# Placing the first expert block ahead of the third pair's last attention outputs, with the first half's gather plan put earlier

## The chip, the core and the metric

One NeuronCore of a Trainium2 chip runs the whole program in one launch. The metric is the device time of that launch in microseconds (us). Five instruction streams run side by side and meet through semaphores: PE (TensorE, matrix products), DVE (VectorE), ACT (ScalarE), POOL (GpSimd, which also issues the indirect transfers) and SP (SyncE, which issues all the other transfers).

## What is computed

Eight batches of 576 tokens go through linear attention with 8 heads, then through a mixture of 8 experts of which each token uses two, then through a soft mixture of experts.

```python
kv = np.einsum('bhsd,bhde->...', softmax(k, over tokens), v)   # per head 64x64
x  = softmax(q, over dims) @ kv                                 # 4608 x 512
...
noisy = x @ w_gate + log1p(exp(x @ w_noise)) * noise            # 4608 x 8
top2, weights = two largest per token, softmax over the two
out[mask] += weight * (relu(x[mask] @ w1[e]) @ w2[e])           # each expert e
...
soft mixture of experts over out                                # second stage
```

The weights `w1[e]` are 512 x 1024 and `w2[e]` 1024 x 512, in float32. A product in float32 is made of three products: each operand is split into a high and a low part, and high x high, high x low and low x high are summed.

## The kernel before

**Attention.** The tokens are taken in four pairs of batches (`i` = 0 to 3), each of nine tiles of 128 tokens (`j` = 0 to 8). The order of the work is written by hand as two tables of short steps. `FIRST` is run before the expert stage, `MIX` is spread over the first nine blocks of the expert stage (`SPREAD = 72` parts, eight parts to a block). A step is two letters and its numbers: `lk`, `lv`, `lq` load; `km` to `ke` make the softmax of k; `kv` forms k^T v and `kb`, `kt`, `ku`, `kw`, `kx` turn it into the tile `KB`; `qm`, `qs`, `qe` make exp(q - max) of three tiles (`qs` on GpSimd, with a `v` behind it on VectorE); `qt` and `qu` transpose one tile of q into `qT`; `ou` is the product of `qT` with `KB` into the PSUM tile `pv`; `os`, `oa`, `ol` or `ov` scale it into `xr` and `lgr`; `st` stores 128 rows into the DRAM table `xtab`; `he` sums the gate logits over the heads. `ga` starts the gate of a pair (or of two) as a background generator, and each `bg` runs one piece of it. The gate ends in `tab`, which holds for every expert the numbers of its tokens.

**Order.** Inside `FIRST` every engine runs its instructions in the order of the table (`tc.manual_schedule`). In `MIX` and in the expert stage a scheduler places the instructions of each engine when the program is built; it may take one ahead of another on the same engine where no data forbids it.

**First half's plan.** After the gates of pairs 0 and 1, `plan_first` (L633) turns the counts and `tab` into the list of rows for the first ten expert blocks: `pl_m` (L594 to L597), the counts (L639 to L654), eight copies on GpSimd into `pl_ia` at places that are read into registers (L656), the expert of each block `pl_eba` (L629) and `pl_done` (L665). Then two indirect transfers (`gather_rows`, L774) fetch the 2 x 128 rows of block 0 into `pl_x0` and `pl_x1`. The second half's plan (`plan`, step `pl`) is the last step of `MIX` but for its `bg`s; its row lists `pl_idx` and `pl_id3` are copied on GpSimd (L735 to L744).

**Expert blocks.** A block is 256 gathered rows and one expert. SP reads the expert's number (`expert`, L814) and loads eight pieces of 512 KB of its weights into `ringS` (L819; u = 0 to 3 are `w1`, 4 to 7 `w2`). Each piece is split by ACT into its high part `R?h` and by DVE into its low part `R?l` (`split`, L827), in three slots R0, R1, R2 taken in turn. `xpose` (L847 to L852) transposes the rows on PE, ACT makes `xh`, DVE makes `xl` and the weight of each row (`sc`). `hidden` (L862) makes 24 products of 256 columns for each of u = 0 to 3, and ACT and DVE make `hh` (L865) and `hl` (L866). `result` (L892) makes 12 products of 512 columns for each of u = 4 to 7. DVE scales the two results into `y` (L897) and GpSimd adds them to `x2` by an indirect transfer (L898). Weights and rows of the next block are fetched during the block; its rows are transposed at u = 6.

PSUM for `pv` has two buffers (`pb`, `pc`) during `FIRST` and one (`pb`) after it; the PSUM of the expert stage takes the place of `pc` and of the three transpose buffers.

Blocks 0 to 9 take rows of the first half. After them come blocks of three tiles (`THREE`) and of two, whose number is read at run time.

Of the kernel before, what the change touches and what calls it, by code (L numbers as in the profile page):

```python
# [59 lines left out]
kv3.1.0 bg st2.5 ke3.0.1 bg kv3.1.1 bg ov2.2 bg ou2.8 bg st2.2 he2.0 bg qt2.3 ov2.8 bg qu2.3 ou2.4 bg st2.8 bg kb3.1 bg kv3.0.0 bg pf bg kt3.1 kv3.0.1 ku3.1 kw3.1 kx3.1 kb3.0 bg os2.4 ou2.7 qm3.0   # L60
oa2.4 kt3.0 ov2.7 ou2.3 ku3.0 st2.4 ol2.4 qm3.1 qs3.0 st2.7 kw3.0 ou2.6 kx3.0 os2.3 qs3.2v oa2.3 qs3.1 ov2.6 qe3.0 st2.3 he2.2v st2.6 ol2.3 qe3.2 he2.1 qe3.1
# [66 lines left out]
def attention(k):  # L128
# [3 lines left out]
    with ExitStack() as ctx:  # L132
# [440 lines left out]
        plain = {"lk": load_k, "lv": load_v, "lq": load_q, "se": setup, "wu": level, "kf": rest_tr, "kg": rest_max, "km": k_max, "kn": km_tr, "ko": km_max, "kp": ms_tr, "ks": k_sub, "ke": k_exp, "qe": q_exp, "qt": q_tr, "qu": q_copy, "kb": kv_out, "kt": kb_tr, "ku": kb_copy, "kw": kb_w, "kx": kw_copy, "ou": out, "os": out_sums, "ol": out_logits, "st": out_store}  # L573
# [59 lines left out]
def plan_first(k, cnt):  # L633

    nc = k.nc
    t = lambda n, s, d=F32: k.ac.tile(s, d, name=n)
    m = table(k)
    pn = k.pt([P, E])
    nc.tensor.matmul(pn, k.ones16, cnt, start=True, stop=True)  # L639
    k.c1 = t("pl_c1", [P, E])  # L640
    nc.vector.tensor_copy(k.c1, pn)
    ti = t("pl_ti", [P, E], I32)
    nc.vector.tensor_copy(ti, pn)
    nc.vector.tensor_scalar(ti, ti, 8, None, op0=ALU.logical_shift_right)
    cf = t("pl_tf", [P, E])
    nc.vector.tensor_copy(cf, ti)
    ru = t("pl_ru", [P, 2, E + 1, E])[:, 0]
    nc.vector.tensor_tensor(ru, bcast(cf, 1, E + 1), k.tri, op=ALU.mult)
    en = t("pl_en", [P, 2, E + 1])[:, 0]
    nc.vector.tensor_reduce(en, ru, axis=AX.X, op=ALU.add)  # L650
    st = t("pl_st", [P, E], I32)
    nc.vector.tensor_scalar(st, en[:, :E], 2.0, None, op0=ALU.mult)
    k.idxa = k.cp.tile([P, TE + TE], I32, name="pl_ia")
    nc.vector.memset(k.idxa, 0)  # L654
    for e in range(E):
        nc.gpsimd.tensor_copy(k.idxa[:, bass.ds(at_register(k, st[0:1, e:e + 1], TE), TE)], m[:, e * TE:(e + 1) * TE])  # L656
    k.eoha = k.cp.tile([P, NPA, E], F32, name="pl_eoa")
# [813 lines left out]
```

## Time and profile before

| | |
|---|---|
| median of 3 runs | 1192.28 us (1190.68 to 1193.77) |
| profiled execution | 1193.88 us, its span 1192.2 us |
| mean granted clock of PE, as a share of full speed | 0.971 |
| PE busy | 1116.4 us, 94% of the span |
| DVE, ACT, POOL busy | 67%, 48%, 28% of the span |
| HBM traffic | 242 GB/s over the span |

The profile is of one execution. A row of a timeline gives the start, the duration, the engine, the line of the kernel, the operation with its output and inputs, the count of instructions merged in the row, and in brackets the idle time before it with what ended it. PE's products in float32 appear as two records each. A `windows` row gives for a stretch the busy time of each engine and how many instructions, PE's granted clock (1.00 is 2.4 GHz, 0.50 is 1.2 GHz), the share of the 16 DMA engines and GB/s.

### The profile page before, as it was taken

What the parts mean: (1) busy time and instruction counts of PE and PEld (TensorE: products, weight loads), DVE (VectorE), ACT (ScalarE), POOL (GpSimd) and SP (SyncE); (2) the same over time, 40 slices, a digit from 0 to 9 for tenths busy, and PEclk for the clock granted to TensorE, in tenths of its full rate; (3) what the DMA queues carried; (4) which work ended last, traced back from release to release, by engine and by line L of the source; (5) the groups of instructions that cost most, each with busy time, mean ns of one, the idle gap of its engine ahead of it and who ended that gap; (6) DMA issues with size and microseconds to landing.
All of it is one profiled execution on the core that took longest, in us unless ns stands there. A gap on an engine that the chain in (4) does not pass through costs nothing. (4 is left out here: it accounts for less than half of the span.)

```text
span 1192.2 us, 21160 instructions
## 1 busy us (share of the span) xinstructions
PE 1116.4 (94%) x7820; PEld 980.2 (82%) x7820; DVE 796.4 (67%) x1390; ACT 567.8 (48%) x873; POOL 334.0 (28%) x361
## 2 busy tenths in 40 slices
PE   3898769999999999999999999999999999999994
PEld 3787758998888998999989899899899899986542
DVE  7899878756996665455556666666666666657653
ACT  3575446454544453444435455545445545534324
POOL 4442152332333332122222332332232232211000
PEclk8899779999999999999999999999999999999997
DMA  9999161867445375666659684746546263557797
GB/s 330 297 315 336 46 213 32 263 192 229 116 104 176 96 217 154 174 164 166 168 129 310 190 216 106 221 92 192 136 126 192 37 196 53 159 163 235 264 353 317
DMA packets 119431, 222.72 MB, mean 187 GB/s; under 512 B 14096, under 2 KB 56208, under 8 KB 115472
## 3 DMA queue, kind: packets, MB, share of 16 engines
q1 hardware_dynamic: 102432, 181.31, 44.5%
q0 software_dynamic: 16880, 39.90, 17.4%
q8 instruction: 65, 1.06, 0.4%
q14 instruction: 54, 0.44, 0.1%
HBM read 238.58 MB, written 49.70 MB: 242 GB/s over the span
## 5 line engine op out<-in xcount | busy, mean ns | idle before, releaser
L827 DVE TENSOR_TENSOR R0l<-ringS,R0h 128x1024 fp32r<-128x1024 f32 x101 | 124.4, 1231 | 100.3 <-ACT R0h L827 100.2
L827 DVE TENSOR_TENSOR R1l<-ringS,R1h 128x1024 fp32r<-128x1024 f32 x102 | 125.1, 1226 | 98.7 <-ACT R1h L827 98.6
L827 ACT ACTIVATE R1h<-ringS 128x1024 fp32r<-128x1024 f32 x102 | 108.2, 1061 | 157.8 <-PE py L892 82.6
L827 ACT ACTIVATE R0h<-ringS 128x1024 fp32r<-128x1024 f32 x101 | 107.2, 1061 | 143.5 <-PE ph L862 69.4
L862 PE MATMUL ph<-xh,R0h 128*128 128x256 f32 x504 | 140.4, 279 | 1.5 <-PEq L994 0.9
L862 PE MATMUL ph<-xl,R0h 128*128 128x256 f32 x504 | 139.9, 278 | 0.0
L862 PE MATMUL ph<-xh,R0l 128*128 128x256 f32 x504 | 139.8, 277 | 0.0
L827 ACT ACTIVATE R2h<-ringS 128x1024 fp32r<-128x1024 f32 x77 | 81.7, 1061 | 101.5 <-PE py L892 57.0
L774 POOL DMA_INDIRECT xg<-xtab,pl_idx x38 | 50.7, 1335 | 258.8 <-DVE sc L852 221.0
L827 DVE TENSOR_TENSOR R2l<-ringS,R2h 128x1024 fp32r<-128x1024 f32 x77 | 94.6, 1229 | 42.2 <-ACT R2h L827 42.0
L866 DVE SCALAR_TENSOR_TENSOR hl<-ph,hh 128x512 fp32r<-128x512 f32 x140 | 95.8, 684 | 19.7 <-ACT hh L865 19.7
L892 PE MATMUL py<-R1h,hl 128*128 128x512 f32 x252 | 99.0, 394 | 0.0
L892 PE MATMUL py<-R1l,hh 128*128 128x512 f32 x252 | 98.9, 393 | 0.0
L862 PEld LDWEIGHTS ph<-xh,R0h 128*128 128x128 f32 x504 | 94.7, 188 | 3.6 <-issue 2.5
L865 ACT ACTIVATE hh<-ph 128x512 fp32r<-128x512 f32 x140 | 81.6, 583 | 31.3 <-PE ph L862 31.3
L862 PEld LDWEIGHTS ph<-xl,R0h 128*128 128x128 f32 x504 | 94.7, 188 | 1.3
L862 PEld LDWEIGHTS ph<-xh,R0l 128*128 128x128 f32 x504 | 94.9, 188 | 0.0
L862 PE MATMUL ph<-xh,R1h 128*128 128x256 f32 x312 | 87.1, 279 | 8.0 <-DVE sc L852 7.6
L892 PE MATMUL py<-R1h,hh 128*128 128x512 f32 x252 | 94.5, 395 | 0.0
L862 PE MATMUL ph<-xl,R1h 128*128 128x256 f32 x312 | 87.0, 279 | 0.0
L862 PE MATMUL ph<-xh,R1l 128*128 128x256 f32 x312 | 86.7, 278 | 0.3 <-DVE R1l L827 0.3
L862 PE MATMUL ph<-xh,R2h 128*128 128x256 f32 x304 | 84.7, 279 | 0.6 <-DVE hl L866 0.6
(465 smaller groups left out, 2901.0 us busy)
## 6 DMA issues: line engine op xcount, KB each, us to landing
ringS<-in_moe_w_dram SPq DMA_DIRECT2D x284, 512.0 KB
ringA<-in_moe_w_dram SPq DMA_DIRECT2D x12, 1024.0 KB
ringA<-in_moe_w_dram SPq DMA_DIRECT2D x22, 512.0 KB
xtab<-xr SPq DMA_DIRECT2D x36, 256.0 KB
kt<-in_k_dram SPq DMA_DIRECT2D x8, 1024.0 KB
v<-in_v_dram SPq DMA_DIRECT2D x8, 1024.0 KB
x<-z SPq DMA_DIRECT2D x5, 1280.0 KB
ringS<-x SPq DMA_DIRECT2D x5, 1024.0 KB
```

The source lines that it names most:

```text
L774: k.nc.gpsimd.indirect_dma_start(out=x, out_offset=None, in_=k.xtab[:n], in_offset=bass.IndirectOffsetOnAxis(ap=idx, axis=0))
L827: turn[1:] = [nc.scalar.activation(r[0], f, AF.Copy), nc.vector.tensor_sub(r[1], f, r[0].bitcast(F32))]
L862: nc.tensor.matmul(ph[:, g, :], w[i][:, c, g * P:(g + 1) * P], x[:, c, :], start=n == 0, stop=n == 11)
L865: nc.scalar.activation(hh[:, fs, :], ph, AF.Relu)
L866: nc.vector.scalar_tensor_tensor(hl[:, fs, :], ph, 0.0, hh[:, fs, :].bitcast(F32), op0=ALU.max, op1=ALU.subtract)
L892: nc.tensor.matmul(py[s], a[h], w[i][:, f, :], start=u == 4 and f == n == 0, stop=u == 7 and f == 1 and n == 2)
```

## The change

- The step `pf` becomes five steps of a class `First`: `pm` (the table), `pc` (counts), `px` (places), `pe` (blocks) and, later, `pg` (the two gathers). They are put behind the gate's last `bg` and `kv3.0.1`.
- Of the third pair's last six outputs only 2.8 and the start of 2.4 stay in `FIRST`; 2.4's scaling, outputs 2.7, 2.3, 2.6, the head sums `he2.1` and `he2.2`, and the fourth pair's `qs3.0`, `qm3.1`, `qs3.1`, `qs3.2` and the three `qe3` become the first 24 steps of `MIX`, which grows from 135 to 159 steps. `qs3.2` and `he2.2` lose their `v` (GpSimd in place of VectorE), output 2.8 goes to VectorE (`ov2.8`).
- A step `sw` turns the two `pv` buffers once, so that the output 2.4 lies in the one that stays.
- In block 0 a new helper `behind` ties instructions to the last one recorded on the engines named, so that they stay in the written order: `MIX` steps on PE, DVE and ACT, the split of piece 1 behind the transposes, and the split of piece 2.

```diff
-kv3.1.0 bg st2.5 ke3.0.1 bg kv3.1.1 bg ov2.2 bg ou2.8 bg st2.2 he2.0 bg qt2.3 ov2.8 bg qu2.3 ou2.4 bg st2.8 bg kb3.1 bg kv3.0.0 bg pf bg kt3.1 kv3.0.1 ku3.1 kw3.1 kx3.1 kb3.0 bg os2.4 ou2.7 qm3.0
-oa2.4 kt3.0 ov2.7 ou2.3 ku3.0 st2.4 ol2.4 qm3.1 qs3.0 st2.7 kw3.0 ou2.6 kx3.0 os2.3 qs3.2v oa2.3 qs3.1 ov2.6 qe3.0 st2.3 he2.2v st2.6 ol2.3 qe3.2 he2.1 qe3.1
+kv3.1.0 bg st2.5 ke3.0.1 bg kv3.1.1 bg ov2.2 bg kv3.0.0 bg st2.2 he2.0 bg qt2.3 
+bg qu2.3 bg bg kb3.1 bg kv3.0.1 bg pm pc px pe kt3.1 ku3.1 ou2.8 kw3.1 kx3.1 kb3.0 kt3.0 ku3.0 kw3.0 kx3.0 ov2.8 sw ou2.4 qm3.0 pg st2.8
...
+            elif a == "sw":
+                pbs.append(pbs.pop(0))
...
+        def behind(*engs):
+
+            stack = ExitStack()
+            for eng in engs:
+                stack.enter_context(tc.issue_after(next(i for i in reversed(nc.cur_bb.bb.instructions) if i.engine == eng.engine)))
+            return stack
...
-                    split(*ahead[u])
+                    with behind(*((nc.vector, nc.scalar) if b == u == 0 else ())):
+                        split(*ahead[u])
...
         split(0, 0)
-        split(0, 1)
         for s in range(2):
             xpose(0, s)
+        with behind(nc.vector, nc.scalar):
+            split(0, 1)
...
-                while n_done < min(n_steps, n_steps * n_parts // SPREAD):
-                    n_done += 1
-                    next(att)
+                with behind(*((nc.tensor, nc.vector, nc.scalar) if b == 0 else ())):
+                    while n_done < min(n_steps, n_steps * n_parts // SPREAD):
+                        n_done += 1
+                        next(att)
```

DVE, between the gate's second and third chunk (`ob`, `oa` are the gate's one-hot tiles; `rqa`, `xr`, `lgr` the scaling of an output); `-` is before, `+` the change:

```order
 L507 TENSOR_TENSOR ob<-ob,tok_112 128x768
 L510 TENSOR_TENSOR oa<-cols,af 128x3x288
-L363 TENSOR_SCALAR rqa<-pv 128x8
-L364 RECIPROCAL rqa<-rqa 128x8
-L376 TENSOR_TENSOR xr<-pv,rqa 128x512
-L377 TENSOR_TENSOR lgr<-pv,rqa 128x128
 L506 TENSOR_TENSOR ob<-cols,bf 128x768
 L507 TENSOR_TENSOR ob<-ob,tok_112 128x768
```

The scaling of output 2.8 has gone from between the gate's chunks; it now stands behind the plan.

PE, around the transposes of block 0's rows (`pl_x`). Before:

```order
L347 MATMUL pv<-KB_130,qT 128x162 x4
L328 MATMUL pt<-ident,KB_131 128x128 x4
L347 MATMUL pv<-KB_129,qT 128x162 x4
L337 MATMUL pt<-wbd,kbT 128x32 x4
L347 MATMUL pv<-KB_130,qT 128x162 x4
L847 MATMUL ph_1781<-ident,pl_x_1642 128x128 x4
L847 MATMUL ph_1790<-ident,pl_x_1643 128x128 x4
L298 MATMUL pt<-ident,qt 128x128 x4
L862 MATMUL ph_1807<-xh,R1h 128x256
L347 MATMUL pv<-KB_131,qT 128x162 x4
L298 MATMUL pt<-ident,qt 128x128 x4
```

and in the change:

```order
L337 MATMUL pt<-wbd,kbT 128x32 x4
L328 MATMUL pt<-ident,KB_131 128x128 x4
L337 MATMUL pt<-wbd,kbT 128x32 x4
L347 MATMUL pv<-KB_130,qT 128x162 x4
L871 MATMUL ph_1710<-ident,pl_x_1655 128x128 x4
L871 MATMUL ph_1719<-ident,pl_x_1656 128x128 x4
L886 MATMUL ph_1738<-xh,R1h 128x256
L886 MATMUL ph_1738<-xl,R1h 128x256
L886 MATMUL ph_1738<-xh,R1l 128x256
L886 MATMUL ph_1738<-xh,R1h 128x256
```

Three of the four outputs (L347) that stood in front of the transposes have gone behind them, and the transposes of q (L298) no longer stand between the first product of block 0 (L862, now L886) and its second.

ACT, in the stretch where k of the fourth pair is exponentiated (`kt`; `qt` here is q of that pair, step `qe3.2`):

```order
 L423 ACT_TABLE_LOAD
 L423 ACTIVATE ln<-g_1217 128x72
+L293 ACT_TABLE_LOAD
+L293 ACTIVATE qt<-qt 128x1536
 L332 COPY kbT<-pt 128x512
-L276 ACT_TABLE_LOAD
 L276 ACTIVATE kt<-kt 128x1024
 L340 COPY KB_129<-pt 128x4x32
```

The scheduler has taken `qe3.2`, a step of `MIX`, into this stretch, and the load of the table of exp with it; on POOL its subtraction `qs3.2` (`L288 TENSOR_TENSOR qt<-qt,qm`) likewise stands one row ahead of the gate's L431.

## Rows read from the trace of the kernel before

**Rows 1.** Busy time in two stretches: us, then each engine, clock, DMA share, GB/s.

```profile
142.40:184.40 42.00, 25.23 (x163) 23.70 (x161) 31.08 (x84) 16.93 (x38) 20.61 (x27) 0.72 0.47 164
184.40:1192.20 1007.80, 983.94 (x6871) 857.64 (x6869) 641.33 (x1059) 472.27 (x663) 260.72 (x244) 0.99 0.60 176
```

**Rows 2.** Timeline of PE.

```profile
171.19 0.66 PE L847 MATMUL ph<-ident,pl_x 128*128 128x128 f32 x4 [0.55 <-ACT xr L374]
...
180.86 0.55 PE L862 MATMUL ph<-xh,R1h 128*128 128x256 f32 x1 [7.63 <-DVE sc L852]
...
184.43 0.39 PE L862 MATMUL ph<-xh,R1l 128*128 128x256 f32 x1
...
189.96 1.26 PE L347 MATMUL pv<-KB,qT 128*128 128x162 f32 x8
```

**Rows 3.** Timeline of DVE, from the gate to the plan.

```profile
144.52 0.15 DVE L363 TENSOR_SCALAR rqa<-pv 128x8 f32<-128x8 f32 x1
...
145.75 0.55 DVE L506 TENSOR_TENSOR ob<-cols,bf 128x768 f16<-128x768 f16 x1
...
151.99 0.31 DVE L519 TENSOR_SCALAR tt<-pk 128x144 f32<-128x144 f32 x1 [3.40 <-PE pk L513]
...
155.30 0.17 DVE L641 COPY pl_c<-pt 128x8 f32<-128x8 f32 x1 [1.35 <-PE pt L639]
```

**Rows 4.** Timeline of SP: the loads of block 0.

```profile
159.19 5.03 SPq L819 DMA_DIRECT2D ringS<-in_moe_w_dram  x8
```

**Rows 5.** Timeline of POOL: the gathers of block 0.

```profile
161.81 1.19 POOL L774 DMA_INDIRECT pl_x<-xtab,pl_ia  x1 [0.91 <-POOL pl_ia L656]
163.29 0.98 POOL L774 DMA_INDIRECT pl_x<-xtab,pl_ia  x1 [0.30 <-issue]
```

**Rows 6.** Tile pl_x, issue to landing.

```profile
DMA to landing us min/median/max: 7.5/7.7/7.9
```

**Rows 7.** Tile xg from 165 to 215 us, issue to landing.

```profile
DMA to landing us min/median/max: 3.4/4.9/6.1
```

**Rows 8.** Timeline of ACT: the high part of the rows.

```profile
177.92 1.14 ACT L848 ACTIVATE xh<-ph 128x512 fp32r<-128x512 f32 x2
```

**Rows 9.** Timeline of DVE: the low part of the second 128 rows.

```profile
180.71 0.69 DVE L849 TENSOR_TENSOR xl<-ph,xh 128x512 fp32r<-128x512 f32 x1
```

**Rows 10.** Busy time in five us, columns as in rows 1.

```profile
125.00:130.00 5.00, 5.00 (x22) 5.00 (x22) 2.66 (x7) 2.90 (x5) 0.00 (x0) 0.50 0.14 52
180.00:185.00 5.00, 4.14 (x18) 4.14 (x19) 3.57 (x15) 3.00 (x9) 1.72 (x5) 0.53 0.02 3
```

**Rows 11.** Timeline of ACT, where k of the fourth pair is exponentiated.

```profile
121.47 1.28 ACT L276 ACT_TABLE_LOAD   x1
```

**Rows 12.** Timeline of PE behind it.

```profile
124.03 1.12 PE L328 MATMUL pt<-ident,KB 128*128 128x128 f32 x4 [1.45 <-ACT KB L340]
```

**Rows 13.** Timeline of DVE behind it.

```profile
127.35 0.17 DVE L363 TENSOR_SCALAR rqa<-pv 128x8 f32<-128x8 f32 x1 [2.27 <-PE pv L347]
...
134.21 0.17 DVE L469 TENSOR_TENSOR cnt<-cnt,c 128x8 f16<-128x8 f16 x1 [1.31 <-PE pk L465]
```

**Rows 14.** Timeline of POOL: the first row behind its idle time.

```profile
119.02 0.34 POOL L431 TENSOR_TENSOR g<-g,g 128x72 f32<-128x72 f32 x1 [6.63 <-DVE g L429]
```

**Rows 15.** Timeline of DVE beside POOL's L288.

```profile
168.91 4.28 DVE L288 TENSOR_TENSOR qt<-qt,qm 128x1536 f32<-128x1536 f32 x1
```

**Rows 16.** Timeline of POOL in the same stretch.

```profile
168.81 2.76 POOL L288 TENSOR_TENSOR qt<-qt,qm 128x1536 f32<-128x1536 f32 x1 [1.39 <-PE pv L347]
```

**Rows 17.** Timeline of POOL: the second half's plan and gathers.

```profile
351.81 0.19 POOL L735 CAST pl_id<-pl_m  x1 [1.63 <-DVE pl_m L597]
...
367.04 0.19 POOL L744 CAST pl_idx<-pl_zt 128x2 f32 x1 [0.28 <-POOL pl_id L741]
...
391.30 0.99 POOL L774 DMA_INDIRECT xg<-xtab,pl_ia  x1 [2.16 <-PE py L892]
...
414.70 1.00 POOL L774 DMA_INDIRECT xg<-xtab,pl_id  x1 [2.15 <-PE py L892]
```

More of the change, by code (lines that the diff above doesn't have):

```diff
@@ L569, in step @@
                 back(1)
+            elif a == "sw":
+                pbs.append(pbs.pop(0))
             else:
                 raise ValueError(st)
[L573 removed]
+        first = First(k, cnt)
+        plain = {"pm": first.table, "pc": first.counts, "px": first.places, "pe": first.blocks, "pg": first.gathers, "lk": load_k, "lv": load_v, "lq": load_q, "se": setup, "wu": level, "kf": rest_tr, "kg": rest_max, "km": k_max, "kn": km_tr, "ko": km_max, "kp": ms_tr, "ks": k_sub, "ke": k_exp, "qe": q_exp, "qt": q_tr, "qu": q_copy, "kb": kv_out, "kt": kb_tr, "ku": kb_copy, "kw": kb_w, "kx": kw_copy, "ou": out, "os": out_sums, "ol": out_logits, "st": out_store}
         with tc.manual_schedule(engines={e.engine for e in (nc.tensor, nc.vector, nc.scalar, nc.gpsimd, nc.sync)}):
@@ L630, in block_loads @@
     return t
[L633 to L657, printed above, removed]
-    eq = t("pl_eq", [1, NPB + 1 + NTR + 1, E])[:, :NPA]
-    block_experts(k, en, NPA, k.eoha, eq)
-    k.eba = block_loads(k, eq, "pl_eba")
-    k.done = t("pl_done", [P, E])
-    nc.vector.tensor_scalar(k.done, en[:, :E], -1.0, float(NPA), op0=ALU.mult, op1=ALU.add)
-    nc.vector.tensor_scalar(k.done, k.done, 0.0, None, op0=ALU.max)
-    nc.vector.tensor_tensor(k.done, k.done, cf, op=ALU.min)
-    yield
-    k.xg0 = [t(f"pl_x{s}", [P, XC]) for s in range(2)]
-    for s in range(2):
-        gather_rows(k, k.xg0[s], k.idxa[:, s:s + 1], NTOK // 2)
@@ new lines, with __init__, table, counts @@
+class First:
+    def __init__(self, k, cnt):
+        self.k, self.cnt = k, cnt
+        self.t = lambda n, s, d=F32: k.ac.tile(s, d, name=n)
+    def table(self):
+        self.m = table(self.k)
+    def counts(self):
+        k, t = self.k, self.t
+        nc = k.nc
+        pn = k.pt([P, E])
+        nc.tensor.matmul(pn, k.ones16, self.cnt, start=True, stop=True)
+        k.c1 = t("pl_c1", [P, E])
+        nc.vector.tensor_copy(k.c1, pn)
+        ti = t("pl_ti", [P, E], I32)
+        nc.vector.tensor_copy(ti, pn)
+        nc.vector.tensor_scalar(ti, ti, 8, None, op0=ALU.logical_shift_right)
+        self.cf = t("pl_tf", [P, E])
+        nc.vector.tensor_copy(self.cf, ti)
+        ru = t("pl_ru", [P, 2, E + 1, E])[:, 0]
+        nc.vector.tensor_tensor(ru, bcast(self.cf, 1, E + 1), k.tri, op=ALU.mult)
+        self.en = t("pl_en", [P, 2, E + 1])[:, 0]
+        nc.vector.tensor_reduce(self.en, ru, axis=AX.X, op=ALU.add)
+        self.st = t("pl_st", [P, E], I32)
+        nc.vector.tensor_scalar(self.st, self.en[:, :E], 2.0, None, op0=ALU.mult)
+        k.idxa = k.cp.tile([P, TE + TE], I32, name="pl_ia")
+        nc.vector.memset(k.idxa, 0)
+    def places(self):
+        k = self.k
+        for e in range(E):
+            k.nc.gpsimd.tensor_copy(k.idxa[:, bass.ds(at_register(k, self.st[0:1, e:e + 1], TE), TE)], self.m[:, e * TE:(e + 1) * TE])
+    def blocks(self):
+        k, t, en = self.k, self.t, self.en
+        nc = k.nc
+        k.eoha = k.cp.tile([P, NPA, E], F32, name="pl_eoa")
+        eq = t("pl_eq", [1, NPB + 1 + NTR + 1, E])[:, :NPA]
+        block_experts(k, en, NPA, k.eoha, eq)
+        k.eba = block_loads(k, eq, "pl_eba")
+        k.done = t("pl_done", [P, E])
+        nc.vector.tensor_scalar(k.done, en[:, :E], -1.0, float(NPA), op0=ALU.mult, op1=ALU.add)
+        nc.vector.tensor_scalar(k.done, k.done, 0.0, None, op0=ALU.max)
+        nc.vector.tensor_tensor(k.done, k.done, self.cf, op=ALU.min)
+    def gathers(self):
+        k = self.k
+        k.xg0 = [self.t(f"pl_x{s}", [P, XC]) for s in range(2)]
+        for s in range(2):
+            gather_rows(k, k.xg0[s], k.idxa[:, s:s + 1], NTOK // 2)
```

4 lines of the change are left out of this document (1 added, 3 removed).

## The prediction

> **What bounds the kernel now.** The table ahead gives PE 94% of the span, so I read first where PE is not busy. The busy time by stages answers that [rows 1]: from 184.40 us to the end PE is busy 983.94 of 1007.80 us at a clock of 0.99, so behind that point the end is set by PE's work. In the 42.00 us ahead of it PE is busy only 25.23, at a mean clock of 0.72; 16.8 us are idle. An idle microsecond taken out there moves the end by one, as long as nothing behind has to wait anew. The timeline of PE then shows what it waits for [rows 2]: the second 128 rows of block 0 are transposed at 171.19, the first product of block 0 starts at 180.86 after 7.63 us of idle time, and the third, the first at full speed, at 184.43; an output and the transposes of a tile of q stand between them. The timelines of DVE, SP and POOL give the way there [rows 3 to 5]: the gate's table (151.99), the counts (155.30), the loads of the weights (159.19), the gathers (161.81 and 163.29), whose rows land 7.5 to 7.9 us after issue [rows 6].
>
> **The change part by part.**
>
> *The plan.* On DVE the scaling of output 2.8 leaves the place ahead of the gate's third chunk: 144.52 to 145.75, 1.23 us. DVE then waited 3.40 us for the gate's last products and 1.35 us for the product of the counts [rows 3]. Both were late because PE stood at output 2.4 for its PSUM buffer; in the new order PE has half of kv3.0 and one transpose in their place, which wait for nothing, and I expect both waits gone. If the second stays, 1.35 us are lost. Sum: 1.23 + 3.40 + 1.35 = 6.0 us earlier for the whole plan, so for the loads (153.2) and the gathers (155.8 and 157.3) too [rows 4, 5]. The store of output 2.8 stood ahead of the loads on SP and now stands behind six of them; it has no reader near.
>
> *The landing.* The gathers still follow the first load by 2.6 us, so I keep 7.5 and 7.9 [rows 6]: 163.3 and 165.2. The nearest other gathers, of block 1 and 2, took 3.4 to 6.1 [rows 7]; that is the lower end, 4.5 us earlier for the second. What four gathers in line do to the first two is not in the trace; I put the upper end as far above 7.9 as the median of those (4.9) lies below it, 3.0 us later.
>
> *From the rows to the first product.* One transpose of 128 rows 0.66 [rows 2], their high part 1.14 / 2 = 0.57 on ACT [rows 8], the low part 0.69 on DVE [rows 9], and 0.2 for three hand-overs (an estimate): 165.2 + 2.1 = 167.3. The splits of the first piece of weights are no bound: ACT has nothing ahead of them, DVE only output 2.8, one maximum of q and its own queue behind the plan.
>
> *PE's work behind that point.* Four outputs and two tiles' transposes, done before 184.43 until now, come later. An output is 1.26 us with its tail, some 1.1 without [rows 2]; a tile's transposes have half as many products of 128 in place of 162 columns, 0.43. Sum 4.4 + 0.9 = 5.3. The rest of the attention's products stand on the same side as before.
>
> *The clock.* Ahead of the block PE will have waited, as before. From 180.86 PE was busy and still read 0.50; 180 to 185 us gives 0.53 [rows 10], and the first product at full speed is that of 184.43. That is 3.6 us at half speed, a loss of 1.8. The stretch of 125 to 130 us reads 0.50 throughout with PE busy, so it can last longer; I take 2.0, with 1.8 and 2.5 as ends.
>
> So the work that PE had done at 184.43 is done at 167.3 + 5.3 + 2.0 = 174.6: **9.8 us earlier**.
>
> *What the scheduler took ahead.* ACT's load of the table of exp, 1.28 us at 121.47 [rows 11], stood between PE's transposes and the copy that PE waited 1.45 us for at 124.03 [rows 12]. It now comes with `qe3.2`, in idle time of ACT. The copy comes 1.28 us sooner, which is the lower end of the gain. PE ran on at 0.50 from there [rows 10], and DVE waited 2.27 and 1.31 us for PE's outputs [rows 13]. With the wait nearly gone I expect the clock to stay up; then both waits of DVE go, 3.6 us, the upper end. The price is POOL's subtraction of `qs3.2`, 2.76 us [rows 16], which falls into 6.63 us of idle time ahead of L431 [rows 14], so POOL itself is not late. DVE may be: its own form of that subtraction took 4.28 us while POOL ran one [rows 15, 16]. In this stretch DVE reads mostly PSUM or one tile; I charge 0.7 us for the small operations with two tiles and take **2.9 us**.
>
> The Trainium skill (SBUF — State Buffer, "Who interferes with whom") says that a VectorE instruction with two SBUF inputs and a GpSimd instruction that reads SBUF exclude each other for the whole instruction; by it the sum would have no gain here at all in the worst order of the two. The 4.28 beside 2.76 agrees with exclusion for that pair.
>
> *New cost in the blocks.* The subtractions `qs3.0` and `qs3.1` now run on POOL during block 0 and at the start of block 1, beside DVE's splits of the weights, which have two tiles as inputs. PE needs the low parts at the start of block 1. Ends 0 and 2 x 2.76 = 5.5; I take **1.5**, since by my count of the queues only the second of them meets a split that PE waits for soon. The outputs in the blocks have one PSUM buffer between them; their scalings (ACT some 2 us, DVE 1.3) end ahead of the next output in the order, so I charge nothing for them; if that cover fails, it costs the rest of a scaling. The transfers of SP that are moved (four stores of outputs) go between loads that are needed a block later.
>
> Sum: 9.8 + 2.9 - 1.5 = **11.2 us**. Against the profiled execution, 1193.88, that is 1182.7; the median of the runs lies 1.6 below it, so I forecast **1181.1**.
>
> **The rivals.**
>
> *Late rows.* The gathers land 3.0 us later, the clock costs 0.5 more and another 1.5 us of waits turn up in the first blocks: 11.2 - 5.0 = 6.2, 1186.1. For it: four gathers stand in line now, and the loads hold the transfer engines; against it: four stores of 256 KB that ran beside them have gone elsewhere.
>
> *POOL shuts DVE out.* Where DVE's operations wait for POOL's whole subtraction, the early gain falls to 2.9 - 2.76 = 0.1, and each of two more in the blocks costs 2.76: 9.8 + 0.1 - 5.5 = 4.4, 1187.9. For it: 4.28 against 2.76 [rows 15, 16]; against it: most of DVE's work in those places reads PSUM, or PE has work queued. This is what the rule of the Trainium skill named above would make of it.
>
> *Early rows.* If the gathers of block 0 land in 3.4 us, the first product comes at 162.8 and the gain is 11.2 + 4.5 = 15.7, 1176.6. Against it: these follow the loads as closely as before.
>
> *Both of the first two* give -0.6: no change, 1192.9.
>
> *Slower: the second plan comes too late.* Now 24 more steps stand ahead of it in `MIX`, over the same 72 parts. Its copies on POOL ran from 351.81 to 367.2, 15.4 us, long ahead of the gathers for the first block of three tiles, the last of which was issued at 414.70 [rows 17]. In the new order the copies stand directly ahead of these gathers, behind the sums of block 7. The rows are needed a block after the tile they overwrite is free, and a block lasts 414.70 - 391.30 = 23.4 us, landing takes up to 6.1, so 17 us of delay are free, less 3 for the issue: 14. From 14 + 11.2 = 25 us of delay on, the kernel is slower than before; two blocks late, 47 us, would give 1181.1 + 33 = 1214. Against it: the copies need only the table, which in the new order is ready in the first third of block 8, so they should end about when the gathers may start.
>
> **How the numbers follow.** The forecast 0.50, late rows 0.19, early rows 0.11, POOL shuts DVE out 0.10, no change 0.06, slower 0.04. The range 1176.5 to 1188.0 takes in all but the last two and half of the early rows. About 0.3%, 3.6 us, is what a measurement can tell from no change. Faster by more than that: 0.50 + 0.19 + 0.11 + 0.10 = 0.90; within it 0.06; slower 0.04.
>
> **What would show it.** Right: DVE has no wait ahead of L519 or L650 beyond 0.5 us; the plan 6 to 9 us earlier; the first load near 150 and the rows' transposes near 160 and 162 (both 2.9 us earlier than above); the first product of block 0 near 164, at a clock of 0.50, and full speed some 4 us on; no new wait of PE over 1.5 us in blocks 0 to 2 and none at the first block of three tiles; PE's clock 1.00 in the stretch that read 0.50 at 125 to 130 us. Wrong: landings over 10 us, DVE's splits over 2 us beside L288, or a wait on `xg` behind block 9. A gain under 4 us would say that the start of block 0 was not what PE lost its time to.

## The result: 1180.77 us, 11.6 us faster

| | before | change |
|---|---|---|
| median of 6 runs | 1192.41 us (1190.68 to 1193.77) | 1180.77 us (1178.63 to 1182.55) |
| ratio of the change to before | | 0.9903, 95% interval 0.9889 to 0.9917 |
| profiled execution, its span | 1193.88, 1192.2 us | 1180.85, 1179.1 us |
| mean granted clock of PE | 0.971 | 0.974 |
| PE busy | 1116.4 us | 1113.2 us |

The forecast was 1181.1 with a range of 1176.5 to 1188.0. The profiled execution of before lies 1.5 us above its median, that of the change at its median, so the two spans differ by 13.1 us where the medians differ by 11.6.

The busy time by stages, columns as in [rows 1], answers to those rows:

```profile
142.40:184.40 42.00, 34.18 (x223) 30.74 (x221) 24.96 (x66) 16.54 (x29) 9.32 (x14) 0.80 0.40 139
184.40:1179.10 994.70, 970.25 (x6786) 846.07 (x6784) 640.04 (x1070) 469.91 (x670) 272.61 (x256) 0.99 0.61 179
```

PE is busy 34.18 of the 42.00 us ahead of 184.40 where it was 25.23, and 13.1 us less are left behind that point. The timeline of PE of the change answers to [rows 2]:

```profile
123.71 0.66 PE L328 MATMUL pt<-ident,KB 128*128 128x128 f32 x4 [0.36 <-ACT KB L340]
...
160.88 2.12 PE L871 MATMUL ph<-ident,pl_x 128*128 128x128 f32 x8 [3.62 <-DMA pl_x<-xtab,pl_ia]
...
163.69 0.58 PE L886 MATMUL ph<-xh,R1h 128*128 128x256 f32 x1 [0.69 <-ACT xh L872]
...
164.80 0.41 PE L886 MATMUL ph<-xh,R1l 128*128 128x256 f32 x1
...
169.66 0.28 PE L886 MATMUL ph<-xl,R2h 128*128 128x256 f32 x1
```

The rows' transposes start at 160.88 behind 3.62 us of idle time that a transfer ended, the first product at 163.69 where it was 180.86, and full speed comes at 169.66 (0.28 us for a product in place of 0.41). The wait at 123.71 is the one of [rows 12], 0.36 in place of 1.45. The timelines of DVE, SP and POOL answer to [rows 3 to 5]:

```profile
144.96 0.31 DVE L519 TENSOR_SCALAR tt<-pk 128x144 f32<-128x144 f32 x1
...
146.84 0.16 DVE L650 COPY pl_c<-pt 128x8 f32<-128x8 f32 x1
...
150.72 3.42 SPq L836 DMA_DIRECT2D ringS<-in_moe_w_dram  x6
...
116.83 2.76 POOL L288 TENSOR_TENSOR qt<-qt,qm 128x1536 f32<-128x1536 f32 x1 [3.67 <-DVE qm L281]
...
153.33 1.18 POOL L791 DMA_INDIRECT pl_x<-xtab,pl_ia  x1 [0.91 <-POOL pl_ia L668]
...
158.31 2.77 POOL L288 TENSOR_TENSOR qt<-qt,qm 128x1536 f32<-128x1536 f32 x1
...
186.87 3.75 POOL L288 TENSOR_TENSOR qt<-qt,qm 128x1536 f32<-128x1536 f32 x1 [11.94 <-DVE qm L281]
```

Neither the gate's table (144.96) nor the counts (146.84) has idle time ahead of it: the waits of 3.40 and 1.35 us are gone. The counts come 8.46 us earlier, the loads 8.47, the gathers 8.48. From the first gather's issue to the transposes it is 7.55 us, as in [rows 6]. Of POOL's three subtractions (L288) the first is `qs3.2` in its new place, the second `qs3.0`, ahead of block 0 too, the last `qs3.1` in block 0.

To follow the gain through the blocks I use one mark: the start of the scaling of a block's result, `y`, on DVE (L897, in the change L921). The **lead** of a run at a block is how much earlier that mark comes than in the profile of before. The mark of block 0 on the timeline of DVE, before and in the change:

```profile
210.65 1.40 DVE L897 TENSOR_SCALAR y<-py,gc 128x512 f32<-128x512 f32 x2
```

```profile
193.26 1.40 DVE L921 TENSOR_SCALAR y<-py,gc 128x512 f32<-128x512 f32 x2
```

| block | 0 | 1 | 2 | 6 | 7 | 9 |
|---|---|---|---|---|---|---|
| `y` of before, us | 210.65 | 237.08 | 263.27 | 367.02 | 390.43 | 437.26 |
| `y` of the change, us | 193.26 | 220.37 | 246.05 | 350.62 | 378.20 | 425.13 |
| lead | 17.39 | 16.71 | 17.22 | 16.40 | 12.23 | 12.13 |

Most of the moved work is not paid where it was moved to, but in block 7: `MIX` is 24 steps longer and now still runs there, so that block takes 27.6 us in place of 23.4. Behind block 9 nothing changes but some 1 us in stages that the change does not touch, which I take for the profile of before being slower than its median.

### The profile page after: what moved, and what is told of

The parts are those of the page before. It is cut to its first block, busy times and chain, and to the rows that moved or that the text cites. A ratio compares the mean times of both kernels' runs of the same rounds, so it can differ in the third digit from the quotient of the medians.

```text
span 1179.1 us, 21154 instructions
## 1 busy us (share of the span) xinstructions
PE 1113.2 (94%) x7820; PEld 976.4 (83%) x7820; DVE 792.0 (67%) x1386; ACT 566.8 (48%) x873; POOL 339.5 (29%) x365
## 5 line engine op out<-in xcount | busy, mean ns | idle before, releaser
L886 PE MATMUL ph<-xh,R0h 128*128 128x256 f32 x504 | 140.4, 278 | 2.9 <-DVE hl L890 1.3
L886 PE MATMUL ph<-xl,R0h 128*128 128x256 f32 x504 | 139.8, 277 | 0.0
L886 PE MATMUL ph<-xh,R0l 128*128 128x256 f32 x504 | 139.6, 277 | 0.0
L886 PEld LDWEIGHTS ph<-xh,R0h 128*128 128x128 f32 x504 | 94.6, 188 | 5.1 <-issue 3.7
L886 PEld LDWEIGHTS ph<-xl,R0h 128*128 128x128 f32 x504 | 94.7, 188 | 1.2
L886 PEld LDWEIGHTS ph<-xh,R0l 128*128 128x128 f32 x504 | 94.9, 188 | 0.0
L886 PE MATMUL ph<-xh,R1h 128*128 128x256 f32 x312 | 88.1, 282 | 1.5 <-DVE hl L890 0.8
L886 PE MATMUL ph<-xl,R1h 128*128 128x256 f32 x312 | 87.8, 281 | 0.1
L886 PE MATMUL ph<-xh,R1l 128*128 128x256 f32 x312 | 87.6, 281 | 0.0
L886 PE MATMUL ph<-xh,R2h 128*128 128x256 f32 x304 | 84.6, 278 | 0.4 <-DVE hl L890 0.4
```

The lines of the kernel that those rows point to most:

```text
L886: nc.tensor.matmul(ph[:, g, :], w[i][:, c, g * P:(g + 1) * P], x[:, c, :], start=n == 0, stop=n == 11)
```

## The experiments

The kernels were timed in three sets of four, in the order of the table, each with its own runs of before (medians 1191.38, 1191.53 and 1190.97 us). So ratios are compared, and leads where a mechanism is asked for. The third set holds the change itself once more.

| run | median, us | ratio to before, 95% | lead at blocks 0, 1, 9 |
|---|---|---|---|
| plan early alone | 1191.49 | 1.0004 (0.9995 to 1.0013) | 11.61, 6.57, 3.28 |
| `qs3.2` pinned | 1191.21 | 0.9996 (0.9984 to 1.0008) | 16.16, 10.05, 3.74 |
| plan put back | 1190.46 | 0.9995 (0.9986 to 1.0004) | 9.30, 8.72, 3.76 |
| PE's waits filled | 1178.45 | 0.9899 (0.9886 to 0.9912) | 19.15, 18.48, 13.64 |
| only `qe3.2` pinned | 1182.52 | 0.9924 (0.9912 to 0.9937) | 15.44, 15.19, 9.96 |
| loads behind a store | 1181.29 | 0.9920 (0.9908 to 0.9933) | 17.90, 17.24, 12.42 |
| without `behind` | 1184.23 | 0.9937 (0.9925 to 0.9950) | 16.76, 17.16, 11.17 |
| subtractions early | 1185.97 | 0.9958 (0.9943 to 0.9973) | 17.42, 14.67, 7.06 |
| loads behind the gathers | 1179.17 | 0.9900 (0.9885 to 0.9914) | 19.87, 19.21, 14.40 |
| the same, waits filled | 1175.84 | 0.9875 (0.9860 to 0.9889) | 21.24, 20.66, 15.56 |
| the change again | 1180.31 | 0.9911 (0.9898 to 0.9924) | 17.60, 17.03, 12.27 |
| one POOL subtraction more | 1184.36 | 0.9951 (0.9936 to 0.9966) | 17.82, 12.88, 7.78 |

A lead says more than a ratio where it is one event, but it is of one execution. The leads at block 9 lie 0.7 to 3.8 us above what the ratios make, in every run, in part since they all go by the one profile of before, which is slower than its median. So runs are compared by the difference of two leads, which agrees with that of their ratios to some 3 us at worst. The two profiles of the change itself have the first product at 163.69 and 164.37, so a time ahead of block 0 is good to some 0.7 us.

### The plan early, the rest as before

```diff
+... pm pc px pe kt3.1 ... ou2.4 qm3.0 pg st2.8
+os2.4 ou2.7 oa2.4 ov2.7 ou2.3 st2.4 ol2.4 qm3.1 qs3.0 ... qe3.2 he2.1 qe3.1
```

The same 24 steps are taken out of the head of `MIX`; `behind` stays.

> The change with the third pair's outputs and the fourth pair's q steps put back in front of block 0 in the order of before; the plan, the loads and the gathers stay early. My theory (plan 6.0 us, table load taken ahead 2.5 to 2.9, outputs behind the block 3.6 to 3.8): the plan comes 6 us earlier than before, the table load is back in its old place, block 0's first product comes 4 to 6 us earlier than the 180.86 us of before, and the time is 1186.4 to 1188.4 us against 1192.4 of before. Rival (the rows were never the bound, DVE's outputs and its 4.28 us subtraction ahead of the weights' low parts were): the first product at 179 to 181 us, the time 1190.4 to 1192.4.

Measured: no change, ratio 1.0004. Yet the first product came at 171.67, 9.2 us earlier than before, more than my theory had asked for. It is still 7.1 us behind the transposes of the second rows (164.58), since DVE has its own form of a subtraction of q ahead of the low part of the rows, beside one of POOL. The timelines of DVE, PE and ACT of this run show that and where the rest went:

```profile
162.66 5.10 DVE L289 TENSOR_TENSOR qt<-qt,qm 128x1536 f32<-128x1536 f32 x1
...
171.67 0.58 PE L887 MATMUL ph<-xh,R1h 128*128 128x256 f32 x1 [6.43 <-ACT xh L873]
...
209.82 0.55 PE L887 MATMUL ph<-xh,R2h 128*128 128x256 f32 x1 [3.48 <-DVE s L459]
...
206.46 0.26 ACT L450 ACTIVATE n<-n 128x72 f32<-128x72 f32 x1 [1.97 <-POOL n L448]
...
206.63 1.04 ACT L845 ACTIVATE R0h<-ringS 128x1024 fp32r<-128x1024 f32 x1
```

In before the logarithm and the exponential of pair 2's gate, each with the load of its table, ran on ACT at 180 to 188 us, around block 0's first product; here the scheduler has spread them over block 0 and into block 1. The last (L450) waits 1.97 us for POOL, which had the two sums of block 0's results (L923) ahead of it, and the split of the next piece stands behind it on ACT (206.63). PE waits 3.48 us, and its clock reads 0.50 from 210 to 213 us. The lead falls by 5.0 us in block 1; the other 3.3 us that it loses up to block 9 I did not follow. So my theory holds at the first product and falls at the end; the rival has the time and not the reason. The early plan is worth its 6 us and more at block 0, and by the ratio all of it is given back behind that, the larger part where the steps of the gate then meet block 1.

### `qs3.2` not taken ahead

```diff
+                with ExitStack() as pin:
+                    if st == "qs3.2":
+                        pin.enter_context(tc.issue_after(...the last instruction on POOL...))
```

> The change with one instruction pinned: the subtraction qs3.2 on POOL may not go ahead of the POOL instruction recorded before it, so it and qe3.2 stay in the expert blocks and the table load of exp stays in front of the exponentials of k. My theory: PE waits 1.45 us for the copy of KB again, its clock reads 0.50 at 125 to 130 us again, DVE waits about 2.3 and 1.3 us for PE's outputs, the whole plan comes 2.5 us later than in the change, and the time is 2.5 to 2.9 us above the change: ratio to before 0.9925 (1183.5 us against 1192.4). Rival (that load was hidden, the clock there costs nothing on the path): as the change, ratio 0.9903.

Measured: ratio 0.9996, so not 2.9 us but all of the gain is lost. Ahead of block 0 it went as expected (the wait at the copy of `KB` 1.45 us again, first product at 165.89, 2.2 us later), but for the counts, which come at 148.33, only 1.5 us later. Most of the rest is lost in block 1. The timelines of DVE, POOL and PE:

```profile
200.17 4.50 DVE L847 TENSOR_TENSOR R0l<-ringS,R0h 128x1024 fp32r<-128x1024 f32 x1 [2.77 <-PE ph L889]
...
200.24 3.33 POOL L288 TENSOR_TENSOR qt<-qt,qm 128x1536 f32<-128x1536 f32 x1
...
205.41 0.36 PE L889 MATMUL ph<-xh,R2h 128*128 128x256 f32 x1 [3.71 <-DVE rqa L363]
```

A split of the weights that takes 1.22 us elsewhere takes 4.50 beside the subtraction, PE waits 3.71 us, and its products take 0.41 in place of 0.28 us from 206.9 to 209.4. This is my rival "POOL shuts DVE out", in a place that I had not looked at, since in the change no subtraction stands in block 1 beside a split.

### Only the exponential pinned

```diff
+            with ExitStack() as pin:
+                if (i, j) == (3, 2):
+                    pin.enter_context(tc.issue_after(...the last instruction on ACT...))
```

> The change with only qe3.2 (ACT) pinned behind the ACT instruction recorded before it; qs3.2 stays early on POOL. So the table load of exp is back in front of the exponentials of k, but no POOL subtraction runs in block 1. Theory A (two prices: the table load 2.5 us ahead of block 0, and the subtraction beside a split of the weights in block 1 some 7 us): PE waits 1.45 us at the copy of KB, first product of block 0 some 2.2 us later than in the change, split R0l at the start of block 1 near 1.2 us instead of 4.50, no wait of PE over 1.5 us in blocks 1 and 2, time 2.5 us above the change, ratio to before 0.9925. Theory B (the whole 10 us hang on the table load and what it shifts): ratio 0.9996 as with both pinned.

Measured: 0.9924, as theory A had it: 1.3 to 2.1 of a thousandth, 1.5 to 2.5 us, above the change (0.9903 and 0.9911), and the lead at block 9 is 2.2 us smaller. No split in block 1 is over 1.5 us. The timelines of PE and DVE, from the gate to block 0:

```profile
141.13 0.55 PE L516 MATMUL pk<-oa,ob 128*128 128x144 f16 x6
...
165.50 0.58 PE L889 MATMUL ph<-xh,R1h 128*128 128x256 f32 x1 [0.69 <-ACT xh L875]
...
148.08 0.16 DVE L653 COPY pl_c<-pt 128x8 f32<-128x8 f32 x1
```

The counts come 0.9 to 1.2 us later than in the two profiles of the change (147.18 and 146.84), the first product 1.1 to 1.8 us later, not 2.2. So the table load ahead of block 0 costs some 1 us at the plan and 1.5 to 2.5 at the end, where the prediction had 2.9, and the larger part of what the pinned `qs3.2` lost is not its.

### One POOL subtraction more

```diff
+            if st == "ga2.1":
+                with tc.issue_after(...behind ol2.3 on POOL...):
+                    q_sub(3, 2, zq, (nc.gpsimd,) * 2)
```

`zq` is a tile of zeros, so the values stay as they are.

> The change with one POOL instruction more: a subtraction of zeros from the q tile of step qs3.2 (128 x 1536, two SBUF inputs), at the place on POOL at which that subtraction stood in the run with qs3.2 pinned, in block 1; nothing waits for it until the transposes of that tile, and the order on all other engines is the change's. Theory A (a POOL subtraction there shuts DVE out, and that, not what was late behind it, cost the 8 us): a split of the weights at 198 to 203 us takes over 4 us, PE waits 3 to 4 us for DVE in block 1, its clock falls, and the time is 5 to 8 us above the change, ratio 0.9945 to 0.997. Theory B (what cost there was the exponentials of q coming late, with another order behind them): within 1.5 us of the change.

Measured: 4.05 us above the change beside it (1184.36 and 1180.31), ratios 0.9951 and 0.9911, and 4.5 us by the lead. The timelines of DVE, POOL and PE, and the busy time in two stretches of block 1 (columns as in [rows 1]), one after the other:

```profile
198.52 4.48 DVE L853 TENSOR_TENSOR R0l<-ringS,R0h 128x1024 fp32r<-128x1024 f32 x1 [2.77 <-PE ph L895]
...
198.58 3.33 POOL L291 TENSOR_TENSOR qt<-qt,zq 128x1536 f32<-128x1536 f32 x1
...
203.75 0.55 PE L895 MATMUL ph<-xh,R2h 128*128 128x256 f32 x1 [3.71 <-DVE hl L899]
```

```profile
198.50:203.50 5.00, 1.54 (x12) 1.30 (x11) 4.98 (x2) 2.38 (x4) 4.93 (x4) 0.98 0.86 195
203.50:206.50 3.00, 2.75 (x13) 2.78 (x14) 2.91 (x7) 0.00 (x0) 1.76 (x2) 0.50 0.75 182
```

One instruction on POOL, with the order of all other engines as in the change and nothing near that waits for it, makes the split 4.48 us long (1.22 in the change run beside it), PE waits 3.71 us (0.44 there), and then runs for 3 us at 0.50, busy 2.75 of them, which costs half of that, 1.4: 3.3 + 1.4 = 4.7, where the lead shows 4.5. Theory A is right in mechanism and a little high in price. The split is longer by 3.26 us, the subtraction lasts 3.33: DVE stands still for nearly as long as POOL works. The Trainium skill (SBUF — State Buffer, "Who interferes with whom") says that a VectorE instruction with two SBUF inputs contends with a GpSimd instruction that reads SBUF, and that the lock is exclusive; here the trace agrees. Both pay: POOL's subtraction takes 3.33 us where it takes 2.76 alone, and DVE, which started 0.06 us earlier, is the one held up longer.

Of the loss with `qs3.2` pinned (8.5 to 9.3 thousandths, 10 to 11 us; 8.4 by the lead) the table load takes 2.2 and the collision 4.5, both by the lead. What is left, 1.7 us by the lead, comes with the late exponentials of that tile and was not taken apart.

### The plan put back

```diff
-... pm pc px pe kt3.1 ku3.1 ou2.8 ... ov2.8 sw ou2.4 qm3.0 pg st2.8
+... kt3.1 ku3.1 ou2.8 ... ov2.8 sw ou2.4 qm3.0 pm pc px pe pg st2.8
```

> The change with the plan's four steps moved back behind output 2.8, kb3.0 to kx3.0 and output 2.4, directly in front of the gathers; outputs stay behind the block. My theory: the product of the counts comes about 8 us later than in the change (behind output 2.4 on PE), loads and gathers with it, and the end moves by as much: 1188.8 us (7 to 10 us above the change), with the landing still 7.5 us behind the issue. Rival (the outputs' place is what counts, the rows have slack): within 3 us of the change, 1180.8 to 1183.8.

Measured: 0.9995. The timelines of DVE and PE:

```profile
154.57 0.15 DVE L650 COPY pl_c<-pt 128x8 f32<-128x8 f32 x1
...
168.94 2.15 PE L871 MATMUL ph<-ident,pl_x 128*128 128x128 f32 x8 [14.93 <-DMA pl_x<-xtab,pl_ia]
...
171.78 0.58 PE L886 MATMUL ph<-xh,R1h 128*128 128x256 f32 x1 [0.69 <-ACT xh L872]
```

The counts come 7.7 us later than in the change, the first product 8.1, and the lead at block 9 is 8.4 smaller: one for one by the profile, while the ratios make it 10 to 11 us. PE is idle for 14.93 us ahead of the transposes. The rows of block 0 have no slack once the outputs are behind the block.

### Without the helper `behind`

```diff
-            for eng in engs:
+            for eng in ():
```

> The change with the helper behind made empty, so the scheduler is free in block 0. In its order an output, two q transposes and their scalings on ACT and DVE stand in front of the first product. Theory A (the pins carry part of the gain): the first product comes at 167 to 169 us instead of 163.7, but with 1.5 us of the moved work done ahead, and the time is 2 to 4 us above the change: 1182.8 to 1184.8. Theory B (the rows' landing covers them, as my sum had it at nothing): within 1 us of the change.

Measured: 1184.23, ratio 0.9937, 2.6 to 3.4 thousandths above the change: 3 to 4 us. The timeline of PE:

```profile
163.67 1.11 PE L298 MATMUL pt<-ident,qt 128*128 128x128 f32 x4 [2.06 <-ACT qt L293]
...
168.08 0.36 PE L886 MATMUL ph<-xh,R1h 128*128 128x256 f32 x1
```

A q tile's transposes, which wait 2.06 us for its exponentials, and an output stand ahead of the first product, which comes at 168.08. Theory A held by the medians, and there the pins, which the prediction did not price at all, carry about a third of the gain. By the lead at block 9 (11.17 for 12.13 and 12.27) it is only some 1 us; the rest of the difference lies behind block 9 in these profiles, where the pins do nothing, so how much they carry stays open between 1 and 4 us.

### The loads held behind a store, and behind the gathers

```diff
-        for u in range(8):
-            load(0, u)
+        load(0, 0)
+        with tc.issue_after(k.last_store.ins):
+            for u in range(1, 8):
+                load(0, u)
```

> The change with the loads of block 0's pieces 1 to 7 ordered on SP behind the store of output 2.8 (154.2 us) instead of six of them in front of it (150.7 to 154.1 us). Theory A (the 7.5 us of landing of block 0's rows is the share of the transfer engines that these loads take): the rows' transposes start 2 to 3 us earlier, near 158.5 us, the first product near 161.5, piece 1 still comes in time, time 2 us below the change, 1178.8 us. Theory B (the landing has a length of its own): transposes at 160.9 as in the change, and the time equal or up to 1.5 us longer because the weights come later: 1180.8 to 1182.3.

Measured: 1181.29, no faster. The timeline of PE shows each theory half right:

```profile
158.48 1.09 PE L871 MATMUL ph<-ident,pl_x 128*128 128x128 f32 x4 [1.96 <-DMA pl_x<-xtab,pl_ia]
...
162.00 1.12 PE L871 MATMUL ph<-ident,pl_x 128*128 128x128 f32 x4 [2.44 <-DMA pl_x<-xtab,pl_ia]
```

The first gather was issued at 153.45 and its rows were there 5.0 us later; the second, issued at 154.93 beside the loads that began at 154.2, took 7.1, and the first product came at 163.81 as in the change. So the loads were held further, behind the second gather's issue (POOL writes one column of the tile that the second load fills):

```diff
+        with behind(nc.gpsimd):
+            nc.gpsimd.memset(S[1][:, 0, 0:1], 0.0)
...
```

> The change with the loads of block 0's pieces 1 to 7 held behind POOL's issue of the second gather (POOL writes one column of piece 1's tile there, and SP keeps its order). Theory A (the second 128 rows still landed late with the loads behind the store because these began at 154.2 us, 0.7 us ahead of the second gather's issue): both transposes of the rows near 158.4 and 159.5 us instead of 160.9 and 161.9, first product near 161.3, 2 us below the change run beside it. Theory B (the second gather waits behind the first on the transfer queues whatever the loads do): second transposes at 161 to 162 and the time within 1 us of the change.

Measured: ratio 0.9900, and earlier rows, as the timeline of PE of this run has them:

```profile
156.94 1.09 PE L871 MATMUL ph<-ident,pl_x 128*128 128x128 f32 x4 [0.80 <-DMA pl_x<-xtab,pl_ia]
...
159.41 1.11 PE L871 MATMUL ph<-ident,pl_x 128*128 128x128 f32 x4 [1.39 <-DMA pl_x<-xtab,pl_ia]
...
161.22 0.58 PE L886 MATMUL ph<-xh,R1h 128*128 128x256 f32 x1 [0.69 <-ACT xh L872]
```

The gathers, issued at 153.01 and 154.49, landed in 3.9 and 4.9 us, the first product came at 161.22, and the lead at block 9 is 2.1 us larger than that of the change beside it; by the medians it is 1.1 us, which the intervals do not tell from nothing. So about half of the 7.5 us of landing was the share of the transfer engines that the loads took. The Trainium skill (DMA: Bandwidth & Descriptors, "SWDGE vs HWDGE vs iDMA") says that transfers issued by GpSimd and by the other engines go into different queues of the same transfer engines, which take turns between them; these landings agree.

### PE's waits filled

```diff
-... ou2.8 kw3.1 kx3.1 kb3.0 kt3.0 ku3.0 kw3.0 kx3.0 ov2.8 sw ou2.4 qm3.0 ...
+... ou2.8 wu10 kw3.1 kx3.1 wu9 kb3.0 kt3.0 ku3.0 wu5 kw3.0 kx3.0 ov2.8 sw ou2.4 wu44 qm3.0 ...
```

> The change with 10, 9, 5 and 44 transposes of the identity into a spare PSUM tile in PE's waits between the transposes of KB and the landing of block 0's rows (results unused). My theory: PE's clock stays at 1.00 where the change reads 0.50 from 152.8 to 169.6 us; the rows' transposes cost 1.1 instead of 2.1 us and some 23 products of block 0 take 0.118 instead of 0.213 us, so 3.3 us below the change: 1177.5 us. Rival (the clock falls anyway, or the added products stand in the way of the real ones): 1180.8 to 1184.

Measured: ratio 0.9899, lead at block 9 1.5 us larger than in the change. The busy time of this run in two stretches, columns as in [rows 1]:

```profile
159.30:163.90 4.60, 2.35 (x14) 1.72 (x15) 2.17 (x8) 2.66 (x4) 1.51 (x1) 1.00 1.04 389
163.90:167.30 3.40, 3.40 (x19) 3.40 (x18) 1.87 (x2) 0.42 (x1) 0.00 (x0) 0.50 0.78 293
```

The clock stayed at 1.00 up to block 0, but between the last added product and the third product of the block PE was busy 2.35 of 4.60 us, and behind that it read 0.50 for 3.4 us. Half of the expected gain went there. With the loads held behind the gathers, 36 in place of the 44 and five more unused transposes behind each tile of rows this last wait is closed too:

> The loads held as in the run of this set with that one edit, and PE given 10, 9, 5 and 36 unused transposes in its waits ahead of the rows, 5 between the two transposes of rows and 5 behind them. Theory A: the clock reads 1.00 from 150 us into block 0 without the fall that it had at 164 us with waits left open, and the products of the first piece take 0.118 us each: 2.5 to 3 us below the run with the loads held alone. Theory B (the clock falls in the waits that stay, or the added products delay the rows' own): within 1 us of the run with the loads held alone.

Measured: 1175.84, ratio 0.9875 (0.9860 to 0.9889), 4.5 us below the change beside it and 15.1 below before. The timeline of PE:

```profile
160.75 0.38 PE L886 MATMUL ph<-xh,R1h 128*128 128x256 f32 x1
...
162.07 0.28 PE L886 MATMUL ph<-xl,R1h 128*128 128x256 f32 x1
...
168.73 0.36 PE L886 MATMUL ph<-xh,R0h 128*128 128x256 f32 x1 [1.50 <-DVE rqa L363]
```

The timeline of ACT, and then the busy time from 150 to 170 us (columns as in [rows 1]):

```profile
163.50 1.06 ACT L844 ACTIVATE R0h<-ringS 128x1024 fp32r<-128x1024 f32 x1 [1.56 <-DMA ringS<-in_moe_w_dram]
...
165.67 1.06 ACT L844 ACTIVATE R1h<-ringS 128x1024 fp32r<-128x1024 f32 x1 [1.11 <-DMA ringS<-in_moe_w_dram]
```

and

```profile
150.00:170.00 20.00, 17.72 (x148) 16.67 (x148) 12.90 (x27) 9.72 (x19) 9.14 (x11) 1.00 0.83 277
```

The clock reads 1.00 from 150 to 170 us and the products take 0.28 us from the start. What is left is a new wait of 1.50 us at the third piece (168.73): the loads held back now land late, ACT waits 1.56 and 1.11 us for two of them, and the relu of the first piece and what DVE does behind it, which PE waits for, come only after those splits. This version is faster than both kernels.

### The subtractions early

```diff
-... ou2.4 qm3.0 pg st2.8
+... ou2.4 qm3.0 pg st2.8 qs3.0 qm3.1 qs3.1
```

> The change with qs3.0, qm3.1 and qs3.1 put back into FIRST directly behind the gathers of block 0, so both subtractions run on POOL while DVE waits for the rows, and none beside DVE's work in block 0. Theory A: the sum of a row's weight (sc) that took 2.13 us beside the subtraction in block 0 takes 0.16, PE's wait of 0.45 us in block 1 goes, and MIX is three steps shorter: 0.5 to 1.5 us below the change, 1179.3 to 1180.3. Theory B (the subtraction now meets the split R1l and the low part of the rows): first product 1 to 2.5 us later, time 1181.8 to 1183.3.

Measured: 1185.97, ratio 0.9958: slower than the change by 4.7 to 5.5 thousandths, far more than either theory. The first product came at 164.75, 1.1 us later, and the lead at block 0 was that of the change. It falls by 2.8 us in block 1 and by 4.9 in block 6, where the change loses 0.7 and 0.9. In block 1 PE is idle for 0.3 us in all, so the fall there is work done earlier; block 7 costs less for it (1.5 us of lead where the change loses 4.2). The timeline of PE in block 6:

```profile
329.20 0.39 PE L886 MATMUL ph<-xl,R1h 128*128 128x256 f32 x1 [1.15 <-DVE xl L873]
...
337.80 0.55 PE L886 MATMUL ph<-xh,R0h 128*128 128x256 f32 x1 [2.51 <-DVE cnt L469]
```

Both theories looked at the moved instructions. What cost was the second of these waits: the first answers to one of 1.27 us that the change has (332.97), but behind the 2.51 us for DVE the clock reads 0.50 for 3.4 us, together some 4. Three steps less in `MIX` bring everything behind them earlier against the blocks, and the gate of pair 3 meets other instructions on DVE; that this is why the wait arose I infer from the order, no run shows it by itself.

## Why the prediction was right, and where it was not

**The bound** was read rightly: the time came from PE's idle time ahead of block 0, and about one for one, as the plan put back shows. But the late rows were only about half of that. In before 9.7 us lie between the transposes of the second rows (171.19) and the first product (180.86), in which DVE had its own subtraction of 4.28 us [rows 15], an output's scaling and three splits ahead of the low part of the rows; in the change it is 1.8 us (161.89 to 163.69). Of the 17.2 us by which the first product comes earlier, 9.3 come from the earlier rows and 7.9 from the cleared DVE and ACT. Either by itself, in the runs with the plan early alone and with the plan put back, brought the first product only 9.2 and 9.1 us earlier.

**The plan.** From the gate's first product on PE to the counts it is 146.84 - 139.88 = 6.96 us in place of 155.30 - 142.40 = 12.90: 5.9 us earlier, forecast 6.0.

**What the scheduler took ahead.** The gate's first product comes 142.40 - 139.88 = 2.5 us earlier, forecast 2.9. The timeline of PE, before and in the change:

```profile
142.40 0.55 PE L513 MATMUL pk<-oa,ob 128*128 128x144 f16 x6
```

```profile
139.88 0.55 PE L513 MATMUL pk<-oa,ob 128*128 128x144 f16 x6
```

But only half of this is the table load. With the load pinned in its old place that product comes at 141.13, 1.3 us earlier than before all the same, and the load taken ahead adds 0.9 to 1.3, near the lower end of the term, 1.28. What gives the other 1.3 us no run shows; the profile of before reads 0.50 from 123 to 133 us, the pinned run only from 124 to 127.5. So this term came out in part by luck, and the reason given for its upper half failed. I expected the clock to stay up at 125 to 130 us; in this profile it does, in the second profile of the same kernel it does not, and the counts come at 146.84 and 147.18 all the same. The busy time (columns as in [rows 1]) of the change:

```profile
125.00:130.00 5.00, 4.23 (x32) 3.79 (x31) 4.86 (x11) 3.01 (x5) 0.00 (x0) 1.00 0.16 57
```

and the change again:

```profile
125.00:130.00 5.00, 5.00 (x23) 4.96 (x22) 4.51 (x11) 2.15 (x3) 0.32 (x1) 0.50 0.15 56
```

**Landing and first product.** Landing 7.55 us as forecast, though I had taken the two landings of before the wrong way round (the first gather's took 7.9 us, the second's 7.5), which put that time 0.4 us too late. The forecast of 167.3 - 2.9 = 164.4 counted the low part of the rows; the second product, the first that needs it, comes at 164.42, and one with the high part alone ran ahead of it at 163.69.

**Clock.** I took 2.0 us. The first product comes 184.43 - 163.69 = 20.7 us before the mark from which my sum ran, the lead at block 0 is 17.4: 3.3 us went in between. Of these 22 products at 0.213 in place of 0.118 us make 2.1, and 0.7 is the time from the first product to the second, which the forecast had counted ahead of the block; the other 0.5 was not taken apart. So the clock cost what I had taken, though full speed came 6.0 us behind the first product and not some 4.

**Moved work and new waits.** Forecast 5.3 + 1.5 = 6.8; the lead falls by 17.39 - 12.13 = 5.3. Between the marks of blocks 0 and 9 PE is idle for 3.5 us where it was 2.7 in before, so the new waits cost 0.8, which leaves 4.5 for the moved work. Of the two subtractions that I charged, `qs3.0` ran at 158.31, while DVE was idle. Only `qs3.1` met DVE, not at a split, and there PE had work:

```profile
188.51 2.13 DVE L876 SCALAR_TENSOR_TENSOR sc<-xg,pl_eoa 128x8 f32<-128x8 f32 x1
```

The sum of a row's weight, 0.16 us elsewhere, took 2.13 beside it; PE's next wait was 0.45 us.

**The sum.** The lead at block 9 is 20.7 - 3.3 - 5.3 = 12.1 us against the profile of before, forecast 11.2, and 11.6 by the medians. These three are differences of the same marks, so that they add up is no proof of the terms.

**The rivals.** Late rows and early rows did not come (7.55 us), though the held loads show that early rows were to be had: 3.9 us. The second plan was late as described: its copies on POOL run from 388.51 up to the three gathers for the first block of three tiles, and the last of these is issued at 407.11 where it was 414.70 [rows 17], 4.5 us later against the blocks when the lead of 12.1 is taken off. PE waits for none of it:

```profile
388.51 1.10 POOL L752 CAST pl_id<-pl_m  x1 [0.99 <-issue]
...
407.11 0.96 POOL L791 DMA_INDIRECT xg<-xtab,pl_id  x1 [0.30 <-issue]
```

POOL shutting DVE out is real and dearer than I priced it, 4.5 us a time and not 2.76, because PE's clock falls behind the wait. It did not come because the scheduler had moved `qs3.2`, which I had priced for its table load alone, and `qs3.0` out of the blocks.

**What the sum hid.** It reads as if each part were worth its own term. The runs say otherwise: without the outputs behind the block, without `qs3.2` ahead of it or without the early plan nothing measurable is left, and without the pins, by the medians, two thirds. The total came out right because all parts were there.

## What to carry to other kernels

When work is moved to open a stage sooner, price the stage's first blocks with the moved work and with the steps that they now meet; a part taken by itself may be worth nothing. An elementwise subtraction on GpSimd belongs in a stretch in which VectorE is idle: beside a two-input operation that TensorE waits for it cost 4.5 us. Small gathers that start a stage go ahead of its large loads (7.5 us of landing fell to 3.9; 2.1 us by the lead, not clear of noise by the medians), and unused products in TensorE's wait ahead of the stage were worth their place here (some 3 us) once they left no wait open up to the first real product.

## What the runs showed that I had not expected

- The same kernel, with the same waits of 0.67 and 0.36 us at 121 to 124 us, read 1.00 in one execution and 0.50 in another at 125 to 130 us. Of the ten profiles here with the table load taken ahead, three stay at 1.00 there and seven fall, for all or a part of the stretch; what decides it stays open.
- A POOL subtraction of 2.76 us lasted 3.33 us (with `qs3.2` pinned, and in the run with one more) and 3.75 us (the change, at 186.87) where it met DVE: the pair costs both engines.
- Of the 5.3 us of lead that the work moved behind block 0's start cost, 4.2 were paid in block 7, 200 us later, since the steps are spread by count.
